# Leftover columns as four 32-row column tiles, one more tile's statistics on ScalarE, and a new order in the first stage

## The chip, the cores and the metric

The kernel runs on one core of a Trainium2 chip. The core has five engines with a queue each: TensorE (PE, matrix products; its weight loads are shown as PEld), VectorE (DVE), ScalarE (ACT), GpSimd (POOL) and SyncE (SP, which here only issues DMAs). They meet through semaphores. The metric is the device time of one execution in microseconds (us): the median before is 494.08 us of 3 runs (494.08 to 494.55).

## The reference

The input x has 2048 rows of 576 columns. A spectral filter comes first, a feed-forward block second, both on a normalised input and both added to it:

```python
def _A_ref(x, w_r, w_i):
    X = jnp.fft.rfft2(x.astype(jnp.float32), axes=(-2, -1))
    X = X * (w_r + 1j * w_i)
    return jnp.fft.irfft2(X, s=(S, D), axes=(-2, -1)).astype(jnp.bfloat16)

def _B_ref(x, w_gate, w_up, w_down):
    return (_gelu(x @ w_gate) * (x @ w_up)) @ w_down

h = x + _A_ref(_layernorm(x), w_r, w_i)
out = h + _B_ref(_layernorm(h), w_gate, w_up, w_down)
```

S is 2048, D is 576, the filter is 2048 x 289, the hidden width of the feed-forward block is 4608.

## The kernel before

Rows lie as 128 partitions of 16 rows each, so that "tile h" (h = 0 to 15) holds row h of every partition: `h_sb[:, h, :]`. The program order of each engine is the order in which the code emits it (a manual schedule); there is no planner. PSUM is used through four buffers of 4 KB a partition (`two`), which are handed out in turn: a new product waits until the buffer of four allocations before has been emptied.

**First stage (the first 22 us).** x comes in six loads (tiles 0-1, 2-3, 4-5, 6-7, 8-11, 12-15), behind them nine of the seventeen filter rows of WR and WI. The layer norm's statistics are made in two ways. On DVE, `sd` emits two bn_stats halves and, one step late, the bn_aggr (`flush`). On ACT, `ln_act` makes a pass for the mean and a pass for the mean square, and `ln_fin` on POOL turns the latter into a variance. Tiles 1, 3, 5, 9 and 11 go to ACT, the other eleven to DVE. `ln_rstd` on POOL makes the reciprocal root for a group of tiles (L137, L138), `minus_means` (L142) the negative means.

`norms(lo, hi)` multiplies the 16-row DFT matrix by a tile's rstd on DVE (FR, L391) and lets TensorE apply it (`row16`): the tile's 576 columns are two halves of 288, each 128 + 128 + 32 columns. The first 256 of each half are combined into sums and differences (L327), with the mean taken away (L334). The 32 leftover columns of each half go through `row16_rest` (L351): per tile four products of 64 output partitions by 128 columns; partitions 0-31 and 96-127 are what is wanted, 32-95 are multiplied by zeros later. `fill` (L316) runs twelve products on TensorE ahead of the first tile, whose result is not used.

ACT evicts pairs of tiles into `Bt` (L361); the leftover columns are evicted four tiles at a time (`evict4`, L367), the first two times on ACT, the last two on DVE. Meanwhile the column DFT matrix DT is made on ACT and DVE (`phases`, `drop_sign`, `col_sin` L408, `mirror` L420), its leftover part is copied to DF (L500, L501), and POOL gathers the mirrored half of the filter (`gather`, L397). The twiddle factors TF of the first two groups (`angle_b`, `angle_s`, `angle_c`, `sine` L278, `cosine` L281, `minus_sine` L284 with the slice `first`) are made early, and SP turns them by a DMA transpose into TI (L287) ahead of the two copies of the gathered filter halves into WR and WI (L504). POOL then halves two columns of WR and WI (L508) and clears the padding of Zt and m (L511, L529). SP also copies pieces of DT to DQ (`load_dq`, L518).

**Spectral stage (22 to 65 us).** For nine groups k of row frequencies: column transform (`f2`, L550, with DF as the leftover step), combination with TF (`f3`, L567 and L568), on DVE the sums (`sum_of`, L600) and the product with the filter (`wmul`: L618 with WR, then with WI; `parts`; Zt, L638 and L639), the inverse of the rows with TI (`i3`, L658), and the inverse of the columns (`inv_cols`, L709, with DQ).

**Feed-forward block (65 us to the end).** Gate and up products (L978) and down products (L1021, L1040), with TensorE busy throughout.

## Time and profile before

| | |
|---|---|
| median of 3 runs | 494.08 us (494.08 to 494.55) |
| the profiled execution | 494.6 us |
| its span | 492.8 us |
| PE busy | 484.7 us (98%) |
| DVE busy | 223.4 us (45%) |
| ACT busy | 158.2 us (32%) |
| POOL busy | 29.5 us (6%) |

A profile row of a timeline reads: start in us from the span's start, length in us, engine, line, operation, what it writes and reads, its shape and the number of instructions merged; in brackets the idle time of the engine ahead of it and what ended that. A row of the chain of waits reads: start, length, what. L550 is line 550 of the kernel. Lengths of TensorE's products overlap, since the products are pipelined; the step from one to the next is read from the starts.

### The profile page before, as it was taken

To read this page: it belongs to the slowest core of one execution; us is meant where nothing else is said; L and a number is where in the kernel's file an instruction comes from. 1 tells how busy PE (TensorE), PEld (TensorE's weight loads), DVE (VectorE), ACT (ScalarE), POOL (GpSimd) and SP (SyncE) were. 2 spreads that over 40 slices of the span, in tenths; PEclk is the share of its full clock that TensorE was granted. 3 is DMA by queue.
4 is the path that set the end of the run, shared out by engine and by line. 5 is a ranking of instruction groups with operands and counts; after the bars stand their busy time and mean duration, and the time that the engine had idled before them with its cause. 6 is when DMAs were issued, how large, how long until landed. Compare 5 with 4: busy or idle time off the path is not lost.

```text
span 492.8 us, 12868 instructions
## 1 busy us (share of the span) xinstructions
PE 484.7 (98%) x5762; PEld 338.9 (69%) x5762; DVE 223.4 (45%) x457; ACT 158.2 (32%) x280; POOL 29.5 (6%) x84
## 2 busy tenths in 40 slices
PE   6999999999999999999999999999999999999997
PEld 3777789875589955555699755555799655555995
DVE  8999774798622177333311345333121333333111
ACT  8899863322210022332200132332110232232000
POOL 8500010011100011000000000000000000000000
PEclk9999999999999999999999999999999999999999
DMA  8838979769970049966720089876600377760000
GB/s 278 234 74 184 246 115 240 165 128 212 223 161 3 3 118 195 192 145 147 152 65 1 37 170 199 174 145 147 143 3 3 92 158 155 150 146 1 14 13 25
DMA packets 89582, 62.35 MB, mean 127 GB/s; under 512 B 23222, under 2 KB 88118, under 8 KB 89526
## 3 DMA queue, kind: packets, MB, share of 16 engines
q1 hardware_dynamic: 89238, 60.34, 57.5%
q0 software_dynamic: 288, 1.18, 0.7%
q8 instruction: 45, 0.74, 0.7%
q14 instruction: 11, 0.09, 0.1%
HBM read 52.65 MB, written 2.36 MB: 112 GB/s over the span
## 4 chain that ended last, share of the span: by engine, by line
PE 95%; ACT 2%; POOL 1%; DMA 1%; issue 0%; DVE 0%; ACTq 0%; POOLq 0%
PE gu L978 57%; PE acc L1021 27%; PE pq_ps L550 2%; PE cs_ps L709 2%; PE acc L1040 2%; PE eo_ps L658 2%; ACT junk L128 1%; PE y_ps L848 1%; PE gh_ps L568 1%; PE gh_ps L567 1%; DMA h_sb<-in_A_x_dram 1%; POOL rstd L138 1%; ACT Bt L361 0%; POOL wm_r L397 0%; PE eo_ps L682 0%
## 5 line engine op out<-in xcount | busy, mean ns | idle before, releaser
L978 PE MATMUL gu<-Bt,wgu 64*128 64x512 bf16 (+1 forms) x2646 | 270.6, 363 | 0.0
L978 PEld LDWEIGHTS <-wgu 64*128 64x128 bf16 x2646 | 151.5, 94 | 115.6 <-issue 0.3
L987 DVE TENSOR_TENSOR P_sb<-g_sb,gu 128x512 bf16<-128x512 f32 (+1 forms) x156 | 100.4, 645 | 140.3 <-ACT g_sb L986 140.3
L986 ACT ACTIVATE g_sb<-gu 128x512 f32<-128x512 f32 (+1 forms) x156 | 88.0, 564 | 193.5 <-PE gu L978 193.5
L1021 PEld LDWEIGHTS <-P_sb 64*128 64x128 bf16 x2160 | 122.2, 94 | 10.9
L1021 PE MATMUL acc<-wd,P_sb 64*128 64x288 bf16 x1440 | 90.9, 283 | 0.0
L1030 DVE TENSOR_TENSOR part<-part,acc 128x576 f32<-128x576 f32 x15 | 11.3, 754 | 112.6 <-ACT part L1029 112.6
L1029 ACT COPY part<-acc 128x576 f32<-128x576 f32 x15 | 9.6, 639 | 122.8 <-PE acc L1021 122.8
L1021 PE MATMUL acc<-wd_a,P_sb 64*128 64x288 bf16 x720 | 46.8, 283 | 0.0
L550 PE MATMUL pq_ps<-DT,Bt 128*128 128x290 bf16 x64 | 12.3, 286 | 0.7 <-ACT Bt L361 0.7
L978 PE MATMUL gu<-Bt,wgu_e 64*128 64x256 bf16 (+1 forms) x162 | 12.5, 305 | 0.0
L873 DVE TENSOR_SCALAR hrow<-h_sb,mv,rstd 128x1152 bf16<-128x1152 bf16 x14 | 12.2, 868 | 0.6 <-POOL rstd L911 0.6
L138 POOL TENSOR_TENSOR rstd<-rstd,mhalf 128x1 f32<-128x1 f32 (+2 forms) x17 | 12.0, 709 | 1.4
L1032 DVE TENSOR_TENSOR h_sb<-h_sb,part 128x576 bf16<-128x576 bf16 x15 | 11.4, 758 | 0.5
L550 PEld LDWEIGHTS <-Bt 128*128 128x128 bf16 x96 | 9.1, 97 | 3.4 <-ACT Bt L361 0.8
L978 PEld LDWEIGHTS <-wgu_e 64*128 64x128 bf16 x162 | 10.3, 94 | 1.2
L137 POOL TENSOR_SCALAR rstd<-mv 128x1 f32<-128x1 f32 (+2 forms) x17 | 4.1, 242 | 116.7 <-DVE mv L123 116.0
L561 ACT CAST pq<-pq_ps 128x580 bf16<-128x580 f32 x16 | 10.5, 666 | 1.2 <-PE pq_ps L550 1.1
L709 PE MATMUL cs_ps<-DQ,EO 58*128 58x290 bf16 x144 | 10.8, 283 | 0.0
L327 PE MATMUL f2t<-FR,h_sb 128*128 128x256 bf16 x64 | 9.2, 273 | 0.6 <-DVE FR L391 0.6
L709 PEld LDWEIGHTS <-EO 58*128 58x128 bf16 x160 | 7.8, 94 | 2.4 <-issue 0.7
L550 PE MATMUL pq_ps<-DF,Bt 128*128 128x290 bf16 x32 | 8.9, 285 | 0.0
(149 smaller groups left out, 283.9 us busy)
## 6 DMA issues: line engine op xcount, KB each, us to landing
wgu<-in_B_w_gate_dram SPq DMA_DIRECT2D x46, 432.0 KB, 5.1
wgu<-in_B_w_up_dram SPq DMA_DIRECT2D x46, 432.0 KB, 6.1
wd_a<-in_B_w_down_dram SPq DMA_DIRECT2D x1, 1728.0 KB
wd<-in_B_w_down_dram SPq DMA_DIRECT2D x1, 1728.0 KB
wd<-in_B_w_down_dram SPq DMA_DIRECT2D x6, 288.0 KB, 7.9
out_dram<-h_sb SPq DMA_DIRECT2D x3, 576.0 KB
h_sb<-in_A_x_dram SPq DMA_DIRECT2D x4, 288.0 KB, 4.3
h_sb<-in_A_x_dram SPq DMA_DIRECT2D x2, 576.0 KB
```

The lines of the kernel that those rows point to most:

```text
L138: G.tensor_tensor(dst[:, sl], dst[:, sl], mhalf[:, sl], ALU.pow)
L550: T.matmul(ps[:, par, 0:JP], lhsT=Bt[:, t, col], rhs=DT[:, t // 2, par] if t < 4 else DF[:, par], start=(t == par), stop=(t == 4),)
L561: copy(pq[c][:, rs].rearrange("p r (j a) -> p r j a", a=2), pq_ps[c][:, :, 0:JP].rearrange("p a (r j) -> p r j a", r=2)[:, rs],)
L658: T.matmul(pv[:, n], lhsT=z[:, a, w].rearrange("p b j -> p (b j)"), rhs=TI[:, ts[k], 1 - a : 3 - a, :], start=(a == 0), stop=(a == 1),)
L709: T.matmul(ps[:, e, 0:JP], lhsT=EO[x][rows, w, 2 * g : 2 * g + 2].rearrange("p h e k l -> p (h e k l)"), rhs=DQ[rows, w] if w or e else DT ...
L873: V.tensor_scalar(hrow[:], h_sb[:, h, :].rearrange("p (r k) -> p r k", k=64).unsqueeze(2).to_broadcast([P, NR, 2, 64]), mv2[:, h, 0:1], rs ...
L978: T.matmul(gu[:, c, 0:n], lhsT=w[rows, r, i * P : (i + 1) * P], rhs=hl[tcnk % 2][rows, r, lo:hi], start=(r == 0), stop=(r == NR - 1),)
L986: A.activation(g_sb, gu[:, 0, 0:n], ACT.Gelu_apprx_tanh)
L987: V.tensor_tensor(p_sb(f)[:, lo:hi], g_sb, gu[:, 1, 0:n], ALU.mult)
L1021: T.matmul(accs[i][:, c, 0:DH], lhsT=p_sb(f)[rows, st * P : (st + 1) * P], rhs=wd[f // NWA][rows, f % NWA, c * DH : (c + 1) * DH], start=( ...
L1030: V.tensor_tensor(part, part, accs[1][:, :, 0:DH], ALU.add)
L1032: V.tensor_tensor(hv, hv, part, ALU.add)
```

## The change

It has these parts:

- Leftover columns: `rests` now handles eight tiles at once. Each tile takes eight products of 32 output partitions by 64 columns, in groups of four that lie side by side on the partitions (0, 32, 64, 96): two halves of columns by two halves of the transform's row outputs. `Bt[:, 4]` so holds half as many columns, DF has two versions (one for the partitions below 64, one for those above), and `evict4` runs twice instead of four times, both on DVE. Half of DF's zeros are written by an ACT pass.
- The third block of DT no longer holds rows 288 and 289, so these two (plus and minus one, and zero) are written to `edge` by memsets and reach DQ by one more DMA in each `load_dq`.
- Tile 13's statistics move from DVE to ACT, with a `ln_fin` of its own. For tiles 1, 3 and 5 ACT's second pass subtracts the mean itself, so that they need no `ln_fin`; the factors in `neg` are set accordingly.
- The order: `first`'s angle operations move behind the scaling of tiles 4 to 7, its sine, cosine, sign change and transpose behind the last leftover eviction; on SP the transpose now stands between the copies of WR and WI. Statistics, scalings, gathers and evictions are emitted in a new order; `FILL` is 11 instead of 12; POOL clears Zt behind both halvings.

```diff
@@ -86,9 +86,9 @@
     nhpib = const("nhpib", -0.5 * PI)
     mhalf = keep.tile([P, H], FP32, name="mhalf")
     V.memset(mhalf[:], -0.5)
-    neg = keep.tile([P, 2], FP32, name="neg")
+    neg = keep.tile([P, 2, H], FP32, name="neg")
     for i in range(2):
-        V.memset(neg[:, i : i + 1], -2.0 + i)
+        V.memset(neg[:, i], -2.0 + i)
     mneg = keep.tile([P, 2, H], BF16, name="mneg")
 
 
@@ -108,7 +108,8 @@
 
     DT = keep.tile([P, 3, 2, 2, JH], BF16, name="DT")
     D3 = DT[:, 2]
-    DF = keep.tile([P, 2, 2, JH], BF16, name="DF")
+    DF = keep.tile([P, 2, 2, 2, JH], BF16, name="DF")
+    edge = Bt[0:2, 4, 8 * P : 8 * P + 4 * JH].rearrange("p (r a j) -> p r a j", r=2, a=2)
     DQ = keep.tile([P, NW, 2, JH], BF16, name="DQ")
     mv = keep.tile([P, H, 2], FP32, name="mv")
     rstd = keep.tile([P, H], FP32, name="rstd")
@@ -122,10 +123,21 @@
         V.bn_stats(st[:, 1, :], h_sb[:, h, DH:D])
         V.bn_aggr(dst[:, h, :], st[:])
 
-    def ln_act(h):
-        for i, fn, sc in ((0, ACT.Identity, 1.0 / D), (1, ACT.Square, 1.0 / D**0.5)):
-            junk = roll.tile([P, D], BF16, name="junk", tag="junk", bufs=2)
-            A.activation(junk[:], h_sb[:, h, :], fn, scale=sc, accum_out=mv[:, h, i : i + 1])
+    ROOT = float(D) ** 0.5
+
+    def act_pass(h, i, fn, scale, bias=0.0):
+        junk = roll.tile([P, D], BF16, name="junk", tag="junk", bufs=2)
+        A.activation(junk[:], h_sb[:, h, :], fn, bias=bias, scale=scale, accum_out=mv[:, h, i : i + 1])
+
+    def act_mean(h):
+        act_pass(h, 0, ACT.Identity, -1.0 / (D * ROOT))
+
+    def act_var(h):
+        act_pass(h, 1, ACT.Square, 1.0 / ROOT, mv[:, h, 0:1])
+
+    def act_sums(h):
+        act_pass(h, 0, ACT.Identity, 1.0 / D)
+        act_pass(h, 1, ACT.Square, 1.0 / ROOT)
 
     def ln_fin(hs):
         sq = roll.tile([P, H], FP32, name="sq", tag="sq", bufs=2)
@@ -142,7 +154,7 @@
         G.tensor_tensor(
             mneg[:, :, lo:hi],
             mv[:, lo:hi, 0].unsqueeze(1).to_broadcast(sh),
-            neg[:].unsqueeze(2).to_broadcast(sh),
+            neg[:, :, lo:hi],
             ALU.mult,
         )
 
@@ -185,7 +197,13 @@
     def iota(t, pattern, base=0, cm=0):
         G.iota(t, pattern=pattern, base=base, channel_multiplier=cm, allow_small_or_imprecise_dtypes=True)
 
-    V.memset(DF[:], 0.0)
+    V.memset(DF[64:128, 0], 0.0)
+    A.activation(
+        DF[0:64, 1].rearrange("p b a j -> p (b a j)"),
+        zerob[0:64].to_broadcast([64, 4 * JH]),
+        ACT.Sin,
+        bias=zerob[0:64],
+    )
     V.memset(DT[:, :, 1, :, JH - 1], 0.0)
 
     iu, ic = tmp("iu", [P, H, 8]), tmp("ic", [P, H, 8])
@@ -204,7 +222,8 @@
     make_identity(nc, ident[:])
     iD = tmp("iD", [P, 3], FP32)
     iota(iD[:], [[P, 3]], 0, 1)
-    iota(iD[64:128, 2:3], [[0, 1]], 2 * P + 64 + 192, 1)
+    for p0, d0 in ((32, 544), (64, 256), (96, 544)):
+        iota(iD[p0 : p0 + 32, 2:3], [[0, 1]], d0, 1)
     iJ = tmp("iJ", [P, 2 * JM], FP32)
     iota(iJ[:], [[1, 2], [2, JM]])
     iDs = tmp("iDs", [P, 3], FP32)
@@ -308,7 +327,7 @@
         V.tensor_scalar(F16[:, 1, :], F16[:, 0, :], -1.0, None, op0=ALU.mult)
 
     ps_f = {}
-    FILL = {0: 12}
+    FILL = {0: 11}
 
     def fill(dst, n):
 
@@ -339,22 +358,21 @@
                 stop=True,
             )
 
-    def rests(h):
-        ps_f["f4", h] = two("f4")
-        for i in range(4):
-            row16_rest(h + i)
-
-    def row16_rest(h):
-        o = (h % 4) * P
-        for mean in (False, True):
-            for p0, d0 in ((0, 256), (64, 512)):
-                T.matmul(
-                    ps_f["f4", h - h % 4][p0 : p0 + 64, 0, o : o + P],
-                    lhsT=mneg[:, 1, h : h + 1].to_broadcast([P, 64]) if mean else h_sb[:, h, d0 : d0 + 64],
-                    rhs=FR[:, h, 0, :],
-                    start=not mean,
-                    stop=mean,
-                )
+    def rests(h0):
+        ps = ps_f["f4", h0] = two("f4")
+        for h in range(h0, h0 + 8):
+            o = (h - h0) * 64
+            for mean in (False, True):
+                for x in range(2):
+                    for n in range(2):
+                        p0, d0 = 64 * x + 32 * n, 256 + DH * n
+                        T.matmul(
+                            ps[p0 : p0 + 32, 0, o : o + 64],
+                            lhsT=mneg[:, 1, h : h + 1].to_broadcast([P, 32]) if mean else h_sb[:, h, d0 : d0 + 32],
+                            rhs=FR[:, h, 0, 64 * x : 64 * x + 64],
+                            start=not mean,
+                            stop=mean,
+                        )
 
     def evict(*hs):
         for h in hs:
@@ -364,9 +382,9 @@
             )
 
     def evict4(h):
-        (V.tensor_copy if h >= 8 else A.copy)(
-            Bt[:, 4, :].rearrange("p (c h l) -> p h c l", c=16, h=16)[:, h : h + 4, :, :],
-            ps_f["f4", h][:, 0].rearrange("p (h c l) -> p h c l", h=4, c=16),
+        V.tensor_copy(
+            Bt[:, 4, 0 : 8 * P].rearrange("p (c h l) -> p h c l", c=8, h=H)[:, h : h + 8],
+            ps_f["f4", h][:, 0].rearrange("p (h c l) -> p h c l", h=8, c=8),
         )
 
     agg = []
@@ -380,11 +398,19 @@
 
 
         for h in hs:
-            st = roll.tile([P, 2, 6], FP32, name="st", tag="st", bufs=3)
-            V.bn_stats(st[:, 0, :], h_sb[:, h, 0:DH])
+            lower(h)
             flush()
-            V.bn_stats(st[:, 1, :], h_sb[:, h, DH:D])
-            agg.append((h, st))
+            upper(h)
+
+    half = {}
+
+    def lower(h):
+        half[h] = roll.tile([P, 2, 6], FP32, name="st", tag="st", bufs=3)
+        V.bn_stats(half[h][:, 0, :], h_sb[:, h, 0:DH])
+
+    def upper(h):
+        V.bn_stats(half[h][:, 1, :], h_sb[:, h, DH:D])
+        agg.append((h, half[h]))
 
     def norms(lo, hi):
         for h in range(lo, hi):
@@ -418,6 +444,9 @@
         for a in range(2):
             dst, src, sg = DT[:, :, a, r, JM - a : JH - a], DT[:, :, a, r, JM - 2 :: -1], sgn[:, r : r + 1]
             V.tensor_scalar(dst, src, sg, None, op0=ALU.mult)
+
+    def copy_filter(w, t):
+        nc.sync.dma_start(w[:, 9 : H + 1, 0:J], t[:].rearrange("p (r j) -> p r j", r=8))
 
     G16v = [G16[:, sign].rearrange("p x q -> p (x q)") for sign in range(2)]
     pt = []
@@ -434,90 +463,99 @@
                     stop=True,
                 )
 
-    for h in (1, 3, 5):
-        ln_act(h)
+    act_mean(1)
+    act_mean(3)
+    act_var(1)
+    act_var(3)
+    act_mean(5)
     row_table()
     sd(0)
     minus_row()
-    sd(2, 4)
+    sd(2)
+    V.memset(edge[:, 1], 0.0)
+    for a in range(2):
+        V.memset(edge[:, 0, a], 1.0 - 2.0 * a)
+    for i in range(2):
+        V.memset(neg[:, i, 1:6:2], (2 - i) * ROOT)
+    sd(4)
     small_table()
-    ln_fin(slice(1, 4, 2))
     ln_rstd(rstd, mv, 0, 4)
     minus_means(0, 4)
+    act_var(5)
+    A.activation(G16v[0], pt[0][:, 0, 0 : 2 * P], ACT.Copy, scale=G_SCALE)
+    for h in (9, 11, 13):
+        act_sums(h)
+    sd(6, 7)
+    flush()
+    ln_rstd(rstd, mv, 4, 8)
+    minus_means(4, 8)
+    gather(0)
+    norms(0, 2)
+    sd(8)
+    norms(2, 4)
+    sd(10)
+    flush()
+    ln_fin(slice(9, 12, 2))
+    ln_rstd(rstd, mv, 8, 12)
+    minus_means(8, 12)
+    norms(4, 6)
+    sd(12)
+    norms(6, 8)
+    rests(0)
+    flush()
+    ln_fin(slice(13, 14))
+    ln_rstd(rstd, mv, 12, 14)
+    minus_means(12, 14)
+    gather(1)
     angle_b(first)
     angle_s(first)
     angle_c(first)
-    sine(first)
-    cosine(first)
-    A.activation(G16v[0], pt[0][:, 0, 0 : 2 * P], ACT.Copy, scale=G_SCALE)
-    for h in (9, 11):
-        ln_act(h)
-    sd(6, 7)
-    flush()
-    ln_fin(slice(5, 6))
-    ln_rstd(rstd, mv, 4, 8)
-    minus_means(4, 8)
-    gather(0)
-    norms(0, 4)
-    rests(0)
-    minus_sine(first)
-    turn_tf(first)
-    sd(8, 10)
-    flush()
-    norms(4, 8)
-    rests(4)
-    ln_fin(slice(9, 12, 2))
-    ln_rstd(rstd, mv, 8, 12)
-    minus_means(8, 12)
-    gather(1)
-    evict(0, 2)
-    evict4(0)
-    evict(4, 6)
-    evict4(4)
-    sd(12, 13)
-    flush()
-    ln_rstd(rstd, mv, 12, 14)
-    minus_means(12, 14)
-    phases(0)
-    norms(8, 12)
-    rests(8)
-    sd(14, 15)
+    evict(0, 2, 4, 6)
+    sd(14)
+    norms(8, 10)
+    sd(15)
     flush()
     ln_rstd(rstd, mv, 14, 16)
     minus_means(14, 16)
+    norms(10, 12)
+    phases(0, 1, 2)
     norms(12, 14)
-    phases(1, 2)
     drop_sign(kd[:], pd[:])
-    norms(14, 16)
-    rests(12)
-    evict(8, 10)
+    evict(8)
     col_sin(1, pd, zerob)
     col_sin(0, kd, hpib)
-    evict(12, 14)
+    evict4(0)
+    norms(14, 16)
+    rests(8)
+    evict(10, 12, 14)
     mirror(1)
     mirror(0)
+    for x in range(2):
+        V.tensor_copy(DF[64 * x : 64 * x + 64, x], D3[64 * x : 64 * x + 64])
     evict4(8)
-    V.tensor_copy(DF[0:32], D3[0:32])
-    V.tensor_copy(DF[96:128], D3[96:128])
-    evict4(12)
-    for w, t in ((WR, wm[0]), (WI, wm[1])):
-        nc.sync.dma_start(w[:, 9 : H + 1, 0:J], t[:].rearrange("p (r j) -> p r j", r=8))
+    sine(first)
+    cosine(first)
+    minus_sine(first)
+    copy_filter(WR, wm[0])
+    turn_tf(first)
+    copy_filter(WI, wm[1])
     angle_a(rest)
     angle_b(rest)
     for w in (WR, WI):
         G.tensor_scalar(w[:, :, 0 : J : J - 1], w[:, :, 0 : J : J - 1], 0.5, None, op0=ALU.mult)
-        if w is WR:
-            for z in Zts:
-                G.memset(z[:].rearrange("p a w b j -> p (a w b) j")[:, :, JW:], 0.0)
+    for z in Zts:
+        G.memset(z[:].rearrange("p a w b j -> p (a w b) j")[:, :, JW:], 0.0)
     def load_dq(r):
         for w in range(1 - r, NW):
             j0, j1 = w * JW, (w + 1) * JW
-            for lo, hi in ((j0, min(j1, (j0 // P + 1) * P)), ((j0 // P + 1) * P, j1)):
+            for lo, hi in ((j0, min(j1, (j0 // P + 1) * P)), ((j0 // P + 1) * P, min(j1, DH))):
                 if lo < hi:
                     p0 = 64 * r + lo - j0
                     nc.sync.dma_start(
                         DQ[p0 : p0 + hi - lo, w], DT[lo % P : lo % P + hi - lo, lo // P, :, r, :]
                     )
+        p0 = 64 * r + DH % JW
+        nc.sync.dma_start(DQ[p0 : p0 + 2, NW - 1], edge[:, r])
 
     load_dq(1)
 
@@ -549,8 +587,8 @@
         for par, t in steps:
             T.matmul(
                 ps[:, par, 0:JP],
-                lhsT=Bt[:, t, col],
-                rhs=DT[:, t // 2, par] if t < 4 else DF[:, par],
+                lhsT=Bt[:, t, col if t < 4 else slice(col.start % (8 * P), col.start % (8 * P) + P)],
+                rhs=DT[:, t // 2, par] if t < 4 else DF[:, slot[c] // 8, par],
                 start=(t == par),
                 stop=(t == 4),
             )
```

## Prediction

> **What bounds the kernel now.** I read the page first, then the chain of waits in order of time, then the timelines of the engines up to 35 us.
>
> ```profile
> span 492.8 us, 12868 instructions
> PE 95%; ACT 2%; POOL 1%; DMA 1%; issue 0%; DVE 0%; ACTq 0%; POOLq 0%
> ```
>
> The chain (start us, length us, what):
>
> ```profile
> 0.72 2.95 DMA h_sb<-in_A_x_dram
> ...
> 18.00 1.06 POOL rstd L138
> ...
> 19.10 0.30 DVE FR L391
> ...
> 33.84 0.28 PE gh_ps L567
> ...
> 38.80 1.09 PE eo_ps L658 x10
> ...
> 65.57 27.46 PE gu L978 x468
> ```
>
> Everything behind 33.84 is TensorE (PE) in one piece, so a shift of that point is the change of the time. Ahead of it lie 34 us in which the engines take turns. The change touches only these, so the question is where three points land: the start of the column transform, its first leftover product, and 33.84. The profiled execution took 494.6 us, 1.8 outside the span, 0.5 above the median of 494.08; I add the shift to the median. Below 0.2%, or 1.0 us, I call it no change, about what a measurement of this kernel can tell.
>
> **1. Statistics of tiles 6 and 7.** Timelines of VectorE (DVE) and GpSimd (POOL):
>
> ```profile
> 1.14 0.54 DVE L188 MEMSET DF<- 128x580 bf16 x1
> ...
> 5.98 0.46 DVE L384 BATCH_NORM_STATS2 st<-h_sb 128x6 f32<-128x288 bf16 x1 [0.52 <-DMA h_sb<-in_A_x_dram]
> ...
> 6.79 0.28 DVE L269 TENSOR_SCALAR pr<-pr 128x256 int32<-128x256 int32 x1
> ...
> 7.64 0.45 DVE L384 BATCH_NORM_STATS2 st<-h_sb 128x6 f32<-128x288 bf16 x1
> ```
>
> ```profile
> 9.72 0.27 POOL L137 TENSOR_SCALAR rstd<-mv 128x4 f32<-128x4 f32 x1 [0.48 <-DVE FR L391]
> ...
> 12.98 0.20 POOL L132 TENSOR_TENSOR sq<-mv 128x2 f32<-128x2 f32 x1
> ...
> 13.55 0.23 POOL L137 TENSOR_SCALAR rstd<-mv 128x4 f32<-128x4 f32 x1
> ```
>
> The three angle operations from 6.79 to 7.64 (0.85 us) move behind later work. The new memsets hold 580 elements of edge (0.54 by the DF row) and four tiny ones; they fill the 0.52 us wait ahead of 5.98 and spill 0.1. DF's own memset keeps its 580 elements a partition; its other half is an ACT pass beside DVE's first work. Tile 6 then waits for its load: chunk one landed at 0.72 + 2.95 = 3.67, chunk three at about 5.97, so chunk four at an estimated 7.1 to 7.3; I take 7.25. POOL's rstd of tiles 4 to 7 follows tile 6's start by 9.72 - 7.64 = 2.08, so it starts at 9.33, 0.39 earlier. Without the angles' move this gain is nil.
>
> **2. POOL's chain, tile 13.** From 9.72 on POOL runs without a stop to the last rstd, which ends at 18.00 + 1.06 = 19.06: two gathers, four rstd. All of it stays, only the second gather sits one rstd later. Tile 13 on ACT takes a statistics step off DVE, but adds a variance fix (L132, L133) to POOL: 13.55 - 12.98 = 0.57 for two tiles, hardly less for one; I take 0.55. The fixes of tiles 1, 3 and 5 vanish, but they lay ahead of 9.72, and two more iotas take their place. The last rstd ends at 19.06 - 0.39 + 0.55 = 19.22, and the scale FR of tile 14 starts at 19.26, 0.16 later.
>
> **3. Last rows and the eviction.** TensorE and ACT:
>
> ```profile
> 19.45 0.38 PE L327 MATMUL f2t<-FR,h_sb 128*128 128x256 bf16 x2
> ...
> 20.50 0.22 PE L334 MATMUL f2t<-FR,mneg 128*128 128x128 bf16 x1
> 20.64 0.25 PE L351 MATMUL f<-FR,h_sb 128*64 128x128 bf16 x2
> ...
> 21.06 0.22 PE L351 MATMUL f<-FR,mneg 128*64 128x128 bf16 x2
> 21.96 0.67 PE L550 MATMUL pq_ps<-DT,Bt 128*128 128x290 bf16 x4 [0.68 <-ACT Bt L361]
> 22.52 0.42 PE L550 MATMUL pq_ps<-DF,Bt 128*128 128x290 bf16 x2
> ```
>
> ```profile
> 7.71 0.49 ACT L278 ACTIVATE TF<-pr,pib 128x256 bf16<-128x256 int32 x1
> 8.11 0.49 ACT L281 ACTIVATE TF<-ab,nhpib 128x256 bf16<-128x256 f32 x1
> ...
> 8.85 0.68 ACT L128 ACTIVATE junk<-h_sb 128x576 bf16<-128x576 bf16 x1
> ...
> 11.53 1.90 ACT L361 CAST Bt<-f2t 128x1024 bf16<-128x1024 f32 x2
> 13.33 0.59 ACT L367 CAST Bt<-f 128x512 bf16<-128x512 f32 x1
> ...
> 18.86 0.68 ACT L408 ACTIVATE DT<-pd,zerob 128x438 bf16<-128x438 f32 x1
> ...
> 19.98 1.93 ACT L361 CAST Bt<-f2t 128x1024 bf16<-128x1024 f32 x2
> ```
>
> Tiles 14 and 15 run from 19.45 to 20.72, 1.27 us. With FR (0.30) from 19.26 they start at 19.6 and end at 20.87. ACT gives up two leftover evictions and, for now, the twiddles, and gains two passes: six from 8.85 at (11.53 - 8.85) / 4 = 0.67 end at 12.87; seven evictions at 0.90 and the column sines (18.86 to 19.98, 1.12) end by 20.3. So ACT is ready, and the last eviction starts at 20.9, as it does now (19.98 + 0.90). The four PSUM buffers turn in a new order: the first leftover set takes the buffer of tiles 0 and 1, free when ACT has evicted them (12.9 to 13.8, about when tile 7 is done), and tiles 14 and 15 take that set's, which DVE empties while it waits for POOL's 19.22; neither ends last. The column transform keeps its 21.96: DVE's gain and ACT's are both swallowed by POOL.
>
> **4. Leftover products.** Now four tiles take 16 products in eight pairs; from the first pair to the last are seven steps, 21.06 - 20.64 = 0.42, 0.06 a pair. After: 64 for eight tiles, in sixteen fours, each product streaming half the columns. Below: 0.03 a four; above: one behind the other at half a pair's step, 0.12 a four. No row has four column tiles at once; I take 0.06, the step of the nearest row. The last set starts 1.19 after its first row (20.64 - 19.45), at 20.79, issues for 16 x 0.06 until 21.75 and ends 0.16 later (0.22 less the step).
>
> ```profile
> 21.77 0.69 DVE L367 CAST Bt<-f 128x512 bf16<-128x512 f32 x1
> 22.50 1.15 DVE L245 SCALAR_TENSOR_TENSOR pr<-q,s2p,ks 128x896 int32<-128x896 f32 x1
> ```
>
> Its eviction runs from 21.95 to 22.64, so the first leftover product starts at 22.67, not 22.52: +0.15. That only two sets are left of four saves switches off the path.
>
> The pairs' step is 0.03 us a product. The Trainium skill, "TensorE: Matmul & The Clock Gate", "Part 3: Packing small matmuls", has tiles of different columns start about 4 ns apart; by that the fours cost what I take or less. The same page, "Wait — 56ns, not 53.3ns?", says starts never come closer than about 25 ns; by that the set takes about 1.6 us (an estimate), and the result is near rival B. The pair rows fit both.
>
> **5. First twiddles.** Sine and cosine (0.40 from start to start) run from 21.8 to 22.69 on ACT, while TensorE makes what ACT copies next, so nothing waits. The sign change on DVE goes between the eviction and the long angle operation: that starts near 22.7, not 22.50.
>
> **6. The filter's second half.** Sync's queue (SP), the DMA issues (KB, us to landing), and who reads them:
>
> ```profile
> 20.11 0.61 SPq L504 DMA_DIRECT2D WI<-wm_i  x1
> 20.83 5.96 SPq L518 DMA_DIRECT2D DQ<-DT  x7
> 30.50 2.87 SPq L287 DMA_TRANSPOSE TI<-TF  x2
> ```
>
> ```profile
> WI<-wm_i SPq DMA_DIRECT2D x1, 578.0 KB, 3.9
> ```
>
> ```profile
> 24.09 0.48 POOL L508 TENSOR_SCALAR WI<-WI 128x34 bf16<-128x34 bf16 x1 [1.30 <-DMA WI<-wm_i]
> ```
>
> ```profile
> 28.17 0.76 DVE L618 TENSOR_TENSOR m<-xab,WI 128x1156 bf16<-128x1156 bf16 x1
> ...
> 30.70 0.46 DVE L639 TENSOR_TENSOR Zt<-zb,za 128x580 bf16<-128x580 bf16 x1
> ```
>
> ```profile
> 31.29 1.25 PE L658 MATMUL eo_ps<-TI,Zt 128*128 128x256 bf16 x10
> ...
> 33.49 0.29 PE L568 MATMUL gh_ps<-pq,TF 128*128 128x289 bf16 x1
> ```
>
> The transpose now waits for the cosine and the sign (22.76), takes 1.43 to issue (half of 2.87), and WI's copy stands behind it: 24.2 instead of 20.11. It lands 3.9 later, 28.1; POOL halves it in 0.08 + 0.48, so DVE's product with WI starts at about 28.7, 0.53 later than 28.17. Today WI is ready at 24.57, 3.6 us early: that cover is spent. Zt ends at 31.69 instead of 31.16, the inverse product starts at 31.73 instead of 31.29, +0.44. TensorE would reach its next wait at 33.61 (33.49 plus a step of 0.12) and sits till 33.84, so 0.23 is absorbed: 33.84 becomes 34.05, **+0.21**. That covers the +0.15 of step 4. The Zt and m memsets of POOL, now behind WI, end some 0.6 after it, about when DVE first reads m.
>
> Queued behind WI: eight DQ loads at 0.85 (one more each time, for edge) instead of seven, so the later transposes start near 31.7, not 30.50. Their first reader is at 38.80, and the weights' reader at 65.57: covered by over 4 us.
>
> **7. FILL.** One warm-up product less ends at 8.8, rows start about 9.4:
>
> ```profile
> 4.05 5.14 PE L316 MATMUL f2t<-h_sb,ident 128*128 128x512 bf16 x12
> ```
>
> 0.43 us for 512 columns is half the later rate (0.22 for the 512 of two row products): the clock rises just about then. At twelve TensorE would be free at 9.2 too: worth nothing by itself.
>
> **Sum.** Steps 1 to 3: 0. Step 4: +0.15, covered by step 6: +0.21. 494.08 + 0.21 = 494.3 (494.8 against the profiled 494.6).
>
> **Rivals.**
> A, the forecast: 493.9 to 494.7. Step 6 has 0 at the low end (issue 1.25, WI in 3.6) and +0.5 if the transpose's own traffic holds WI.
> B, other side: the fours run serially. The last set takes 64 x 0.03 = 1.92 instead of 0.96; leftover eviction, first leftover product and sign change all come 0.96 later, so do the transpose and WI, and 33.84 moves by 0.21 + 0.96 = 1.2: 495.3. For it speaks that no row packs four; against it that pairs start together and then step by what one product streams. It decides at 0.11 us a four, where the shift reaches 1.0.
> C, POOL is not the last: if the load comes at 7.1 and the fix costs 0.45, 0.25 is won; if also WI comes in time, the end is 493.7. ACT alone would allow 20.3 instead of 20.9, so the floor is -0.6. Hence 1.0 faster has no mechanism in these rows.
> D, the clock: the gap between fill and rows keeps the half rate for another stretch, rows cost 1.1 instead of 0.55. TensorE has about 1.5 us of idle time ahead of tile 14 by step 3, ACT's evictions slip 0.35: 494.6.
>
> **How the numbers follow.** A 0.60, C 0.16, B 0.10, D 0.06, others 0.08, half of them slower by over 1.0 and half faster. The predicted time is A's. The range goes from just under C (493.6) to B (495.3). A, C and D stay within 1.0: the same 0.82; slower is B and half of the others, 0.14; faster the other half, 0.04.
>
> **What would show it.** FR of tile 14 near 19.25, the column transform near 21.95, leftover fours 0.03 to 0.06 apart, WI's halving on POOL ending near 28.6 with DVE waiting for it, and 33.84 near 34.0. Wrong would make it: fours over 0.11 apart, a WI landing far from 28.1, or POOL waiting somewhere in its chain.

## The result and the profile after

The changed kernel takes 495.5 us (median; 495.09 to 496.4) beside 494.52 (494.08 to 495.29) for the kernel before on the same chip: a ratio of 1.0023, 95% interval 1.0015 to 1.0032. (Here and below the ratio is the one on record, with its interval; it is not the quotient of the two medians.) The forecast was 494.3 with a range of 493.6 to 495.3, so the change costs about 1.0 us where 0.2 was expected. The profiled execution after took 495.52 us.

The page after, its span and the row of busy times; then the same row before:

```profile
span 493.7 us, 13000 instructions
...
PE 484.3 (98%) x5825; PEld 338.4 (69%) x5825; DVE 222.9 (45%) x459; ACT 159.8 (32%) x283; POOL 29.1 (6%) x84
```

```profile
PE 484.7 (98%) x5762; PEld 338.9 (69%) x5762; DVE 223.4 (45%) x457; ACT 158.2 (32%) x280; POOL 29.5 (6%) x84
```

TensorE is busy for 0.4 us less and the span is 0.9 longer: TensorE stands still somewhere. Row by row the first stage after came out near the forecast (rows of the timelines of DVE, POOL and PE, in order of time; start, length, engine, line, what, and in brackets the idle time ahead):

```profile
7.25 0.46 DVE L409 BATCH_NORM_STATS2 st<-h_sb 128x6 f32<-128x288 bf16 x1 [0.29 <-DMA h_sb<-in_A_x_dram]
...
18.32 0.72 POOL L150 TENSOR_TENSOR rstd<-rstd,mhalf 128x2 f32<-128x2 f32 x1
...
19.42 0.39 PE L346 MATMUL f2t<-FR,h_sb 128*128 128x256 bf16 x2 [0.39 <-DVE FR L417]
...
20.62 0.21 PE L369 MATMUL f<-FR,h_sb 128*32 128x64 bf16 x4
...
21.09 0.22 PE L369 MATMUL f<-FR,mneg 128*32 128x64 bf16 x4
...
21.80 0.67 PE L588 MATMUL pq_ps<-DT,Bt 128*128 128x290 bf16 x4 [0.49 <-ACT Bt L379]
22.30 0.41 PE L588 MATMUL pq_ps<-DF,Bt 128*128 128x290 bf16 x2
...
27.87 0.42 POOL L545 TENSOR_SCALAR WI<-WI 128x34 bf16<-128x34 bf16 x1 [7.48 <-DMA WI<-wm_i]
...
28.33 0.77 DVE L656 TENSOR_TENSOR m<-xab,WI 128x1156 bf16<-128x1156 bf16 x1 [0.27 <-POOL WI L545]
...
31.42 1.25 PE L696 MATMUL eo_ps<-TI,Zt 128*128 128x256 bf16 x10
```

The first inverse product comes at 31.42 (31.29 before), and TensorE takes that up: its first y product comes at 58.10 (58.14 before). Up to there nothing is lost in this execution. Then, on the chain of waits of after and of before:

```profile
64.25 0.81 PE y_ps L886 x9
65.06 0.49 issue
65.55 0.65 PE y_ps L886 x7
66.20 3.82 PE gu L1016 x69
```

```profile
64.29 1.28 PE y_ps L848 x16
```

Sixteen products that ran in one piece break after the ninth. TensorE stands 0.49 us, for no semaphore: "issue" is time in which an engine waits for nothing that the profile shows. The gate products start at 65.94 instead of 65.31 (timeline), 0.63 later, and all behind them keeps that. At the very end another 0.28 us go: SP's waits before (first row) and after (second row), in us in total, times, longest:

```profile
SPq L1095 <- DMA out_dram<-h_sb: 0.9, 1, 0.9
```

```profile
SPq L1133 <- DMA out_dram<-h_sb: 1.2, 1, 1.2
```

So the path cuts well into four stretches. For each profile below: tile 6's first statistics; the first y product; from there to the first gate product; from there to the start of the last down product; from there to the end of the span. The kernels' names are explained in the next section.

```
                          tile 6   y first   y to gate   gate to last   last to end   span
before                      7.64     58.14        7.17         424.19          3.31   492.81
after                       7.25     58.10        7.84         424.21          3.59   493.74
e12 (after, again)          6.89     57.68        7.84         424.21          3.59   493.32
e16 (after, third)          7.45     58.32        7.24         424.21          3.59   493.36
e17 (after, six loads)      7.88     58.70        7.84         424.21          3.30   494.05
e2  (after, fewer products) 7.57     58.40        7.15         424.19          3.60   493.34
e8  (after, wd_a late)      7.71     58.53        7.15         424.20          3.60   493.48
e3  (before, more products) 7.61     58.02        7.17         424.19          3.30   492.68
e6  (before, late weights)  7.21     57.63        7.15         424.19          3.58   492.55
e7  (before, both)          7.23     57.63        7.23         424.20          3.58   492.64
e18 (before, two loads)     7.82     58.23        7.14         424.19          3.59   493.15
```

The fourth stretch is constant to 0.02 us. The loss is made of the third (0.67, in three of four profiles of the change) and the last (0.28), and the first two have a share that differs from execution to execution.

**Where the stop comes from.** The page's row of DMA queues says what the profile has on instructions (queue, kind: packets, MB, share):

```profile
q8 instruction: 45, 0.74, 0.7%
```

45 packets of 0.74 MB are 16 KB each. TensorE has 2 x 5825 = 11650 instructions (a product and a weight load each), about 256 for each packet, and the stops of e4 below lie 256 instructions apart. So I take it that this is TensorE's stream of instructions, in blocks of 256. By the packet records, the packet of a block starts about when TensorE crosses into the block ahead of it: over the 45 blocks of after, from 2.0 us before the crossing to 5.2 after it. I take it that the crossing is what asks for the next block; that is inferred, not recorded. In after TensorE crosses at 57.71, the packet runs from 62.94 to 64.32, and TensorE goes on at 65.55. The DMA queues in two windows of after, 57.5 to 62.9 (first row, the only queue) and 62.9 to 63.1 (second row), show how late the packet starts:

```profile
q1 hardware_dynamic: 1614, 1.52, 110.7%
```

```profile
q8 instruction: 1, 0.02, 43.2%
```

In before TensorE crosses at 61.54, the packet runs from 62.43 to 63.75, and the block is needed at 68.36. Two things changed: the block ends lie elsewhere, since the change has 126 more TensorE instructions; and the packet starts 5.2 us after the crossing instead of 0.9, and the weights come later. SP's queue after, then before:

```profile
22.57 1.32 SPq L306 DMA_TRANSPOSE TI<-TF  x1
24.00 0.63 SPq L449 DMA_DIRECT2D WI<-wm_i  x1
24.67 6.19 SPq L554 DMA_DIRECT2D DQ<-DT  x7
...
31.69 2.97 SPq L306 DMA_TRANSPOSE TI<-TF  x2
...
40.17 0.72 SPq L171 DMA_DIRECT2D wgu<-in_B_w_gate_dram  x1
...
46.33 1.71 SPq L807 DMA_DIRECT2D wd_a<-in_B_w_down_dram  x1
```

```profile
37.90 0.70 SPq L159 DMA_DIRECT2D wgu<-in_B_w_gate_dram  x1
...
43.78 1.66 SPq L769 DMA_DIRECT2D wd_a<-in_B_w_down_dram  x1
```

The weights' loads leave 2.3 to 2.6 us later. What that does to the traffic, by stretches of 2 us (the last two columns are DMA share and GB/s), after and then before:

```profile
58.00:60.00 2.00, 2.00 (x38) 1.56 (x34) 1.53 (x4) 0.50 (x1) 0.00 (x0) 1.00 1.09 355
...
62.00:64.00 2.00, 2.00 (x51) 1.59 (x49) 1.34 (x6) 2.00 (x5) 1.04 (x2) 1.00 1.12 200
```

```profile
58.00:60.00 2.00, 2.00 (x37) 1.66 (x33) 1.50 (x2) 0.55 (x1) 0.00 (x0) 1.00 0.89 207
...
62.00:64.00 2.00, 1.96 (x50) 1.58 (x46) 1.34 (x6) 2.00 (x5) 1.07 (x2) 1.00 0.21 35
```

Before, the DMA engines were nearly idle when the block was fetched; after, they are full. The packet records say more about what the fetch stands behind. `wd_a` is 1536 packets of 1152 bytes, and the two early loads `wgu_e` behind it are 1152 packets of 768 bytes. In all four profiles of the change (after, and e12, e16 and e17 below) the block's packet starts 0.07 to 0.31 us after the last packet of `wd_a` has ended. In e7, e13 and e15 it starts 0.8 to 0.9 us before that end, with nine or ten packets of `wd_a` to go. In e8, without `wd_a` in this stretch, it starts when 1087 of the 1152 packets of `wgu_e` have started. In e3 and e5 it starts 0.65 to 0.8 us after the crossing, with at most 49 of them started, though in e5 the engines are full (a share of 0.98 from 58.45 to 59.10). So full engines alone do not delay a block; it was late where these loads stood ahead of it. By what rule it gets its turn is not recorded.

The Trainium skill, "Runtime: NRT & Kernel Launch", "Instruction fetch mechanics", has the instructions refilled in 16 KiB blocks of 256 by the sequencer's own DMA queue, and calls the cost mostly hidden; the packets agree with the first, and this case shows one that is not hidden.

### The profile page after: what moved, and what is told of

It is laid out like the page before. It is cut to its first block, busy times and chain, and to the rows that moved or that the text cites. A ratio compares the mean times of both kernels' runs of the same rounds, so it can differ in the third digit from the quotient of the medians.

```text
span 493.7 us, 13000 instructions
## 1 busy us (share of the span) xinstructions
PE 484.3 (98%) x5825; PEld 338.4 (69%) x5825; DVE 222.9 (45%) x459; ACT 159.8 (32%) x283; POOL 29.1 (6%) x84
## 4 chain that ended last, share of the span: by engine, by line
PE 94%; DVE 3%; ACT 2%; DMA 1%; SPq 0%; issue 0%; POOL 0%; ACTq 0%
PE gu L1016 57%; PE acc L1059 27%; PE cs_ps L747 2%; PE acc L1078 2%; PE eo_ps L696 2%; PE pq_ps L588 2%; PE y_ps L886 1%; DMA h_sb<-in_A_x_dram 1%; PE gh_ps L606 1%; PE gh_ps L605 1%; ACT Bt L379 1%; DVE FR L417 1%; DVE st L409 1%; DVE st L412 0%; ACT pq L599 0%; ACT TF L297 0%
```

## Experiments

Times of the kernel before, measured alongside, stand beside each median.

**e1: wd_a later.** The first theory: the stop at 65 us is made by the weights' traffic. In the changed kernel the load of `wd_a` moves behind the second early gate load.

```diff
                     pre = [load_gu(g) for g in range(3)]
-                    nc.sync.dma_start(wd_a[:], wd_view[:, 0:NWA, :])
...
     pre.append(load_gu(4, early[:, 1]))
+    nc.sync.dma_start(wd_a[:], wd_view[:, 0:NWA, :])
```

> The changed kernel with one edit: the 1.7 MB load of the down weights (wd_a) is issued behind the last early gate load, near 66 us, and not near 46 us. Theory (instruction stream): the 0.5 us in which TensorE waits for nothing shown, at 65.06 in the products y_ps, is its next block of instructions, whose fetch was asked for at 57.7 and began only at 62.9 behind the weights' traffic. With that traffic gone the fetch begins within about 1 us of the asking and the stop is gone: 0.65 us faster than the changed kernel, about 494.8, ratio to before about 1.0005. Rival (a wait for data or a buffer at y_ps, or the first stage): nothing changes, 495.5, ratio 1.0023.

Measured 500.14 (before 494.36), ratio 1.0108 [1.0092, 1.0123]. The stop is gone (y to gate 7.15), but the chain has a new wait:

```profile
74.97 5.96 DMA Bt<-hrow
```

The transposes of the next rows now stand behind `wd_a` on SP's queue. The theory holds for the stop; the time was missed, because I moved a load into the way of another.

**e2: fewer products.** The changed kernel without the mean's products of the leftover columns (64 products fewer; the mean is not taken away from these columns).

```diff
-            for mean in (False, True):
+            for mean in (False,):
...
-                            stop=mean,
+                            stop=True,
```

> The changed kernel without the products that take the mean away from the leftover columns (the leftover columns keep their mean): 64 products and 64 weight loads less, so that TensorE has 11,524 instructions and not 11,652, two fewer than before. Weights and queues as in the changed kernel. Theory, form a (the 126 more instructions put a block's end into the crowded stretch): the stop at 65 is gone, 494.8. Form b (the weights' traffic, some 2.5 us later than before, meets the fetch wherever the block's end lies): a stop of 0.3 to 0.8 us stays somewhere from 55 to 70, 495.3. Rival (data): the stop stays at 65 in y_ps, 495.5.

Measured 494.88 (before 494.36), ratio 1.0003 [0.9994, 1.0012]; no stop, y to gate 7.15, though the weights are as late as in after. With other block ends (and 64 products less work) the packet ends over 2 us ahead of its need in this profile, and the stop is gone.

**e3 and e4: one side each in the kernel before.** e3 adds 126 TensorE instructions ahead of everything; e4 puts four repeated loads on SP ahead of the gate weights.

```diff
-    FILL = {0: 12}
+    FILL = {0: 10}
...
+        if h == 0:
+            for i in range(65):
+                q = 32 * (i % 4)
+                T.matmul(f2t[q : q + 32, b, 0:64], lhsT=ident[:, q : q + 32], rhs=h_sb[:, 0, 0:64], start=True, stop=True)
```

```diff
                     load_dq(0)
+                    for _ in range(4):
+                        nc.sync.dma_start(DQ[0:JW, 1], DT[JW : 2 * JW, 0, :, 0, :])
```

> The kernel before with 126 more TensorE instructions and nothing else: two of the twelve warm-up products are replaced by 65 products of 32 partitions by 64 columns in the same stretch ahead of the first row tile. Theory, form a: a block's end moves into the products y_ps as in the changed kernel, and TensorE stops there: 0.3 to 0.7 us slower than before, ratio 1.0006 to 1.0014. Form b: the traffic lies where it lay, the fetch comes in time: no change, ratio within 0.0004 of 1. Rival (data): no change.

> The kernel before with four more DQ loads (each the same small piece again) ahead of the gate weights on SP's queue, so that the gate weights and wd_a are issued some 2.5 us later, as in the changed kernel; TensorE's instructions are those of before. Theory, form a: no stop, ratio within 0.0004 of 1. Form b: a stop of 0.3 to 0.7 us between 55 and 70, ratio 1.0006 to 1.0014. If only both together make the stop, neither this run nor that with more instructions shows it.

e3: 494.49 (before 494.36), ratio 1.0003 [0.9994, 1.0012]. TensorE crosses at 57.52, as in after, but the packet starts 0.8 us later, and there is no stop: the instructions alone cost nothing. e4: 498.86, ratio 1.0088 [1.0073, 1.0104]. Its loads waited for each other, so the weights came 8.4 us later instead of 2.5, more than meant. It shows the blocks all the better, on its chain of waits:

```profile
66.29 3.16 PE gu L980 x56
69.45 1.32 issue
70.77 7.16 PE gu L980 x128
77.93 0.89 issue
78.82 7.16 PE gu L980 x127
85.97 0.09 issue
```

Between stops without a semaphore lie 128 products, with their weight loads 256 instructions: block ends. The stop at 69.45 stands ahead of TensorE's 731st product, and so do those of after, e12 and e17, where that product is one of y_ps and not of gu: the count decides, not the work.

**e5: SP's queue moved forward in the changed kernel.** The gather ahead of tile 13's fix, WI's copy ahead of the transpose, and the edge pieces of DQ from POOL's queue.

```diff
     rests(0)
+    gather(1)
...
-    gather(1)
...
-    turn_tf(first)
     copy_filter(WI, wm[1])
+    turn_tf(first)
...
-        nc.sync.dma_start(DQ[p0 : p0 + 2, NW - 1], edge[:, r])
+        nc.gpsimd.dma_start(DQ[p0 : p0 + 2, NW - 1], edge[:, r])
```

> The changed kernel with SP's queue put forward: the second gather on POOL ahead of tile 13's variance, WI's copy ahead of the first transpose, and the two edge pieces of DQ issued from POOL's queue and not from SP's, so that the gate weights and wd_a are issued within 0.7 us of where they were before the change. TensorE's 11,652 instructions stay. Theory (the stop needs both, the block's end at the y_ps products and the later weights): fetch in time, no stop at 65; DVE does not wait for WI; 494.3 to 494.6, ratio to before 0.999 to 1.0005. Rival (instruction count alone): the stop stays, ratio 1.0012 or more.

Measured 495.33 (before 494.61), ratio 1.0011 [1.0003, 1.002]. No stop (the packet starts 0.65 us after the crossing), and the end takes 3.31 us. But the gather ahead of the last rstd holds up tile 14, whose rows start at 20.27 instead of 19.42; from tile 6 to the first y product it takes 51.21 us, 0.36 more than in after. A wash: one cost was exchanged for another.

**e6 and e7: late weights, and both, in the kernel before.** e6 puts four tiny independent loads ahead of the gate weights (they leave at 40.45); e7 adds e3's instructions.

```diff
                     load_dq(0)
+                    for j in range(4):
+                        nc.sync.dma_start(lag[:, j], DT[0:2, 0, 0, 0, 0:JM])
```

> The kernel before with four tiny loads (2 partitions by 146 bytes, each to its own place, none waits for another) ahead of the gate weights on SP's queue, so that the weights are issued some 2.6 us later; TensorE's instructions as before. Theory (both needed): no stop above 0.2 us, ratio within 0.0006 of 1. Rival (late weights alone do it): a stop at some block's end between 55 and 80, 0.4 us or more, ratio 1.0010 or more.

> The kernel before with both: 126 more TensorE instructions in the warm-up and the weights some 2.6 us later; nothing else of the change. Theory (both needed): TensorE stops 0.4 to 1.0 us in the y_ps products near 65, ratio 1.0010 to 1.0022, the changed kernel's loss made without the change. Rival (something else in the changed kernel): no stop, ratio within 0.0006 of 1.

e6: 495.13 (before 494.61), ratio 1.0014 [1.0006, 1.0023]. e7: 495.22, ratio 1.0018 [1.001, 1.0027]. Each is slower, e6 against the theory that both sides are needed; and neither profile shows a stop, e7's against the same theory. Both profiles, though, were of their kernel's fastest execution.

**e13, e14 and e15: more profiles of e7 and e6.** No edit.

> The kernel before with 126 more TensorE instructions and the gate weights' loads some 2.5 us later, profiled a second time (its first profile was of its fastest execution and had a margin of 1.44 us and no stop). Theory that the median's 0.6 us is the instruction stream's stop: a typical execution (around 495.2) shows a stop without a semaphore of 0.2 to 1 us on TensorE between 57 and 66 us, 256 instructions apart from the other block ends. Rival, that late weights cost something else: no such stop, and the lost 0.6 us stands at another place of TensorE's row.

> The kernel before with the gate weights' loads some 2.5 us later and no more TensorE instructions but the loads' own, profiled a second time. Stream theory: in an execution near its median of 495.1 a stop of 0.2 to 1 us at a block end between 57 and 69 us. Rival: none there, and the time lies elsewhere.

> The same kernel as in e13, a third profile: stream theory a stop at the same instruction as in e13 if the execution is near 495.2, none if it is near 494.4; rival: time and stop have nothing to do with each other.

495.12, 494.89 and 494.69 (before 494.33), and no stop in any: y to gate 7.17, 7.15 and 7.22. So my theory that a late block slows e6 and e7 has no profile for it, and both sides put into the kernel before did not bring the stop back in three profiles. What these five profiles share is the end: 3.57 to 3.59 us instead of 3.31. The rest of their spread is the start: the first y product comes at 57.63 to 58.39, 50.40 to 50.42 us behind tile 6's statistics each time. In the three profiles of e7's kernel the block is just in time: the packet ends 1.35 to 1.44 us ahead of need, and where TensorE did stop it went on 1.2 to 1.6 us after the packet's end.

**e16: a third profile of the change** (e12, further down, is the second).

> The changed kernel, a third profile: stream theory the stop at the same place as in the two profiles so far (behind instruction 1473 of TensorE, 64.5 to 66 us), 0.3 to 0.8 us long, with a time of 495.1 to 495.7; if the stop is missing, a time near 494.7.

495.14. Against the expectation there is no stop as long as 0.3 (timeline of TensorE):

```profile
64.40 1.44 PE L886 MATMUL y_ps<-cs,G 64*128 64x288 bf16 x16
```

The packet ended at 63.92, 0.40 earlier than in after's first profile, and the block was used 1.25 us later; y to gate is 7.24, so some 0.1 was lost. The stop comes and goes. The time is not the 494.7 expected without a stop either: the first y product came late, at 58.32.

**e17 and e18: the end.** In the last rows of every trace SP waits for its transfers' semaphores one after the other, six waits about 0.06 us apart, and the last store's semaphore stands first in after and last in before. The theory is that eight semaphores are used in turn, so that the number of SP's transfers (152 before, 154 after) decides. The traces bear out the turn: SP's transfers carry eight semaphore numbers, one after the other, in every profile. e17 adds six tiny loads to the changed kernel, e18 two to the kernel before, behind the second chunk's last tiles, with no reader (they left at 247 us).

```diff
+        if tcnk == 1:
+            for j in range(6):
+                nc.sync.dma_start(lag[:, j], wd_view[0:2, 0, 0:8])
         if tcnk < 3:
```

> The changed kernel with six tiny loads more on SP's queue half-way through (behind the second chunk's last tiles, about 275 us), which nobody waits for. Theory: the eight semaphores of SP's transfers are used in turn, and the wait for the last store stands first of the six waits at the end because 154 transfers are two more than a multiple of eight; with 160 it stands last, as in the kernel before. So the end behind the last matmul takes 3.31 us instead of 3.59 and the median falls by 0.28 although there is more work. Rival, that the end is longer because of the number of SP's instructions or of the transfers as such: 3.59 or more. TensorE's stop at 65 us is not touched by it.

> The kernel before with two tiny loads more on SP's queue at the same place (154 transfers, as in the changed kernel). Theory of the turn of the semaphores: the end behind the last matmul takes 3.59 us instead of 3.31, the median rises by 0.28, nothing else moves. Rival: 3.31, no difference.

The end takes 3.30 in e17 and 3.59 in e18, both as the theory says. SP's waits in e17 and e18:

```profile
SPq L1137 <- DMA out_dram<-h_sb: 0.9, 1, 0.9
```

```profile
SPq L1099 <- DMA out_dram<-h_sb: 1.2, 1, 1.2
```

Six more loads make the end shorter. The medians go the same way, 494.9 for e17 (ratio 1.0008 [0.9999, 1.0017]; the plain change had 1.0023 and 1.0021) and 494.87 for e18 (before 494.53; 1.0011 [1.0, 1.0022]), but 0.28 us is less than these intervals are wide; the traces carry it. e17's profile has the stop again (y to gate 7.84).

**e8: wd_a behind the transposes.** The changed kernel with `load_wd(0)` in the place of `load_wd(1)`, and that one later.

```diff
-                    nc.sync.dma_start(wd_a[:], wd_view[:, 0:NWA, :])
...
+    todo.setdefault(4, []).append((load_wd, 1))
...
-        2: [(norm2, 3), (flip, 3), (load_wd, 1)],
+        2: [(norm2, 3), (flip, 3), (load_wd, 0)],
```

> The changed kernel with wd_a's load issued behind the two row flips near 74 us, and the next 1.7 MB of down weights two blocks later, so that it meets neither the fetch at 58 us nor the flips. Theory: no stop at 65 and none at the flips, 494.7, ratio 1.0004; a fetch near 75 to 90 may be late instead, with 0.3 us at most. Rival (the stop at 65 is not the traffic): it stays, ratio 1.0023.

Measured 495.03 (before 494.61), ratio 1.0006 [0.9998, 1.0015]. No stop, and no new wait as in e1. What stays, 0.42, is not clear of no difference; it fits the 0.28 of the end and a little at the start.

**e9 and e10: the start, on top of e8.** e9 moves the angle operations back ahead of the statistics of tiles 6 and 7; e10 lets ACT centre tile 13 itself, so that POOL's fix goes.

```diff
     minus_means(0, 4)
+    angle_b(first)
+    angle_s(first)
+    angle_c(first)
```

```diff
+        V.memset(neg[:, i, 13:14], (2 - i) * ROOT)
...
-    for h in (9, 11, 13):
+    for h in (9, 11):
         act_sums(h)
+    act_mean(13)
+    act_var(13)
...
-    ln_fin(slice(13, 14))
```

> The kernel with wd_a behind the flips, and one part of the change undone: the three angle operations of the first twiddles stand ahead of tile 6's statistics again. Theory (the first stage now starts from the landing of tiles 6 and 7's load, and POOL's chain carries it through one to one): tile 6 starts near 7.9 whatever the landing (it landed between 6.3 and 7.7 in the profiles so far), so the third inverse product comes 31.35 behind that, near 39.2: slower than the kernel with wd_a behind the flips by 0.2 to 0.6, ratio to before about 1.0012. Rival (the first stage is bounded elsewhere): no change against the kernel with wd_a behind the flips, ratio about 1.0006.

> The kernel with wd_a behind the flips, and tile 13's second ACT pass takes the mean away itself, as for tiles 1, 3 and 5, so that POOL's variance fix of tile 13 (about 0.6 us of its chain) goes; ACT's pass gets some 0.1 to 0.2 longer. Theory (POOL's chain is last in the first stage): the third inverse product comes 0.2 to 0.6 earlier for the same landing of tile 6's load (less than 31.2 behind it), 494.3 to 494.6, no slower than before. Rival: no change, ratio about 1.0006.

e9: 495.36 (before 494.51), ratio 1.002 [1.0011, 1.0029]; four of its eleven executions, 495.81 to 496.66, have a granted clock of 0.997 where the others have 0.999 or 1.0, so its time says less than its trace. Its load landed at 7.09, but tile 6 starts at 8.05, and the first y product comes at 58.65. DVE's timeline shows the cover that was put back:

```profile
7.84 0.30 DVE L251 TENSOR_SCALAR ab<-ab 128x256 int32<-128x256 int32 x1
8.05 0.45 DVE L409 BATCH_NORM_STATS2 st<-h_sb 128x6 f32<-128x288 bf16 x1
```

e10: 494.66, ratio 1.0006 [0.9997, 1.0015]; from tile 6 to the first y product 50.72, 0.10 less than e8's 50.82. The fix was priced at 0.55; without it the path gets only 0.10 shorter, so something else ends right behind POOL. What that is was not followed up.

**e11: e8's edit in the kernel before**, and **e12: the changed kernel once more.**

> The kernel before, with only the down weights' loads moved behind the row flips. Theory (some executions of the kernel before, too, meet a late fetch near 60 us): the median falls by 0.1 to 0.3, ratio 0.9994 to 0.9998, and the highest runs come down. Rival (only the changed kernel meets it): ratio within 0.0003 of 1.

> The changed kernel as it is, as the standard for the three others on the same chip, and a second profile of it. Theory: the stop at the block's end in the y_ps products is there again, 0.3 to 0.8 us, ratio 1.0018 to 1.0026. Rival (the first profile showed a chance event, the loss is the first stage): no stop, and the third inverse product 0.5 or more later than before's 38.64.

e11: 494.12 (before 494.51), ratio 0.9996 [0.9987, 1.0005], the lowest median of all experiments, but not clear of no difference. e12: 495.37, ratio 1.0021 [1.0012, 1.003]: the loss is confirmed, with the stop at the same instruction (64.64 to 65.13).

## Why the prediction was wrong

- **Step 1** held in this profile: tile 6 at 7.25 as forecast, POOL's rstd at 9.34 for 9.33. That the load landed just there is luck: over 20 profiles it landed at 6.33 to 7.95. Before, tile 6 waited for whichever came last, the landing or the angle operations (tile 4's start plus 1.66); after, for the landing or, where that is early (e1, e12), for tile 4's own statistics (its start plus 0.80). e9, with its landing at 7.09 and tile 6 at 8.05, shows the angles' cover that the move takes away.
- **Step 2** had the mechanism and over-sized it: the last rstd ended at 19.04, not 19.22. The fix took 0.60 (14.80 to 15.40 on POOL), near its price, but the power in the last rstd took 0.72 and not the 1.06 carried over from before. Behind tile 6 the path to the first y product is 0.41 longer in the changed kernel (50.79 to 50.87, where nine of the ten profiles with the old first stage have 50.40 to 50.50).
- **Step 3** held: the column transform came at 21.80 for 21.96. But ACT was free for its last eviction only at about 20.6, not 20.3 (the one before began at 19.73, and they step by 0.90), just ahead of the rows (20.70).
- **Step 4:** the fours step by 0.03 (16 from 20.62 to 21.09), the low bound, not 0.06. The leftover product came at 22.30 instead of 22.67; rival B is out.
- **Step 5** held: nothing waits for the twiddles.
- **Step 6, WI:** halved by 28.29 instead of 28.6, DVE waits 0.27, TensorE absorbs all of it in this profile. Over the profiles the start's net is near the forecast +0.21: the first y product comes at 58.27 on the mean of seven profiles (after, e1, e2, e8, e12, e16, e17) and at 58.06 on that of nine (before, e3, e6, e7, e11, e13, e14, e15, e18), each set spread over 0.8 to 1.0 us. Such means cannot prove 0.2, and the match is partly luck: tile 6 starts 0.20 earlier on these means, not 0.39, and the path behind it is 0.41 longer, not 0.60.
- **Step 6, the queue, is the step that failed:** "Their first reader is at 38.80, and the weights' reader at 65.57: covered by over 4 us." The forecast of the queue was right (later transposes at 31.69 for 31.7), and the readers were covered. But the later loads have another victim: they fill the DMA engines when TensorE's next block of instructions is due, and the stop costs 0.67 in three of four profiles. e2 (other block ends) and e8 (no `wd_a` in that traffic, as in e1, e9 and e10) each remove it; e3 shows that the instructions alone don't make it. That both together suffice is not shown: e7's kernel had both and did not stop. I had read nothing of the q8 row, and took my "Everything behind 33.84 is TensorE (PE) in one piece" as a promise that only a semaphore can break it.
- **The missing term:** the DQ load more each time, for edge, was costed as time in the queue. It also moves the last store to another semaphore, +0.28 at the end, which e17 and e18 switch off and on.
- **Rival C** gave 493.7; the 0.25 that it names takes 494.08 only to 493.8.

Start 0.2, stop 0.5 (0.67 three times and 0.07 once), end 0.28: 1.0, the measured loss; the start's 0.2 is the least sure of the three. **Open** stays by what rule the packet gets its turn: in e8 it waits 4.2 us (58.03 to 62.26) with `wd_a` gone, behind nearly all of the early gate loads, while in e3 it starts 0.8 us after the same crossing, ahead of nearly all of them. Open is also what makes e6 and e7 lose 0.24 to 0.33 beyond the 0.28 of the end. Their slowest executions (496.79 and 497.11, with a granted clock of 0.996 where all others have 0.999 or 1.0) weren't profiled; a stop in them is possible and not shown.

## What to carry to other kernels

When a change delays transfers, ask for their readers, and also who shares the DMA engines at the new time. Here TensorE's own instructions came the same way, and the number of TensorE's instructions ahead decided at which moment. A saving at the head of a kernel of 1 us or less should be checked at its end too, where the number of a queue's transfers alone can be worth 0.3 us. Start a first step at the landing of its load only if you are ready to take that landing's spread.

## What the hardware showed unexpectedly

- TensorE's instructions came in blocks of 256, one 16 KB packet each, over the same DMA engines as the data. In after, most packets started within 2 us of the crossing into the block ahead, those in the weights' traffic up to 5.2 us after it; where a block came at the last moment, TensorE went on 1.2 to 1.6 us after the packet's end.
- Four 32-column tiles side by side start 16 fours of products within 0.47 us (20.62 to 21.09), 0.03 a four, with none of the serial start that rival B feared.
- The same load of x, early in the kernel, landed at 6.33 to 7.95 over the 20 profiles, and at 6.93, 7.95 and 7.33 in three executions of one kernel (e7, e13, e15): a spread of 1.0 us, as much as the whole change is worth.
